# One attention-and-MLP kernel on one core: the weights are loaded and cast by GpSimd-issued DMAs instead of being staged in fp32 and cast by the engines

## The chip, the cores and the metric

The kernel runs on one core of a Trainium2 chip. The metric is the device time of one execution in microseconds (us), and less is better. A core has five engines that each run their own instruction queue in order: TensorE (PE in the profile; its weight loads are shown as PEld), VectorE (DVE), ScalarE (ACT), GpSimd (POOL) and SyncE (SP). Sixteen DMA engines move data between HBM and the on-chip memory SBUF. PSUM holds the results of matmuls.

## The reference: what is computed

Inputs are q, k, v of 8 batches x 8 heads x 576 tokens x 64 dimensions, and two weights, w_in (512 x 2048) and w_out (2048 x 512), all fp32. The output is 4608 x 512 fp32.

```python
# attention, per batch and head: two parts that are added
q_d, k_d, v_d = means over groups of 4 tokens          # 144 pooled tokens
out_up    = repeat(softmax(q_d @ k_d.T / 8) @ v_d, 4)  # every group's result for its 4 tokens
mask      = abs(i - j) < 4
out_local = softmax(where(mask, q @ k.T / 8, -1e9)) @ v
x = (out_up + out_local) as (4608 tokens, 512)
# dense part
h = x @ w_in
out = (h - tanh(h)) @ w_out
```

## The kernel before, in words

**Attention** works on pairs of heads: 8 batches x 4 pairs = 32 pairs, numbered p = 0 to 31. For a pair, q and k land in `qkn` (four buffers) and v lands in `vst` (five buffers), both fp32. `prep_v` (L351) casts v into `vw`. Two casts (L416) reorder q and k into `qr`; TensorE transposes them (L441, for p below 16) and ACT copies the result into `qk` (L445). Pooling of q and k is two additions (L457 into `half`, L462 into `qkd`). The scores come in two groups of matmuls (L476 with `qk`; L492 with the pooled `qkd`), ACT takes the exponentials (L509, L519, L522), DVE applies the mask (L512, L525). `pool_v` (L389, L391, copied out at L396 into `vd`) pools the v of two pairs at once, so it needs `vw` of both. Then `outs` (L536, L543) multiplies with v, DVE normalises (L552, L554 into `ln`), TensorE transposes back (L564 to L568), ACT copies the pooled part (L595 into `od`), and DVE adds the two parts into `xT` (L597).

**The dense part** works on 9 blocks of 512 tokens. `mm1` multiplies a block of `xT` with w_in, 16 column chunks of four matmuls each (L617); ACT takes tanh (L625), DVE subtracts (L628 into `gT`). `mm2` multiplies `gT` with w_out (L644), ACT copies out (L655), SP stores. The first block needs `xT` of all four pairs of batch 0, so no matmul of the dense part can start before the attention of pairs 0 to 3 is done.

**The weights** are cut in eight pieces of 1 MiB (fp32), four of w_in and four of w_out. Piece f of w_in is 128 x 4 x 512: 512 columns of all four row blocks, which is what chunks 4f to 4f+3 of `mm1` read. `load_w` (L324 to L346) has SP load a piece into a stage, a part of the SBUF that `gT` and `xT` will use later, and then four casts (L344) bring it as bf16 to `w_in_sb` or `w_out_sb`. Two of the w_out pieces are loaded by four DMAs each. The order of the SP queue is: q, k and v of pairs 0 to 3, the four w_in pieces, then a pair and a w_out piece in turn.

**The order of the work** is made by a planner in the kernel (`Program`). Each step is entered with an engine, an estimated time, what it reads and writes, and a priority; a step may be offered to several engines (`choice`). `order` plays this through and writes out a fixed order for each engine. So a step that is taken out or given another engine can move other steps: to another place in a queue or to another engine. The offers that matter here are the casts of v (`CAST_V`) and of q and k (`REORDER`), where POOL, ACT and, for q and k, DVE can take the first four pairs. SP has at most eight loads under way, because a load waits for the one eight places before it.

Where TensorE has nothing else to do before the dense part, the planner puts in filler matmuls (L800).

Of the kernel before, what the change touches and what calls it, by code (L numbers as in the profile page):

```python
# [8 lines left out]
FP32 = mybir.dt.float32  # L9
# [6 lines left out]
class Program:  # L16
# [18 lines left out]
    def op(self, eng, ns, fn, reads=(), writes=(), pri=0):  # L35
        i = len(self.ops)
        deps = set()
        for key in reads:
            if key in self.last_write:
                deps.add(self.last_write[key])  # L40
        for key in writes:
            if key in self.last_write:
                deps.add(self.last_write[key])
            deps.update(self.readers.get(key, ()))
        for key in reads:
            self.readers.setdefault(key, set()).add(i)
        for key in writes:
            self.last_write[key] = i
            self.readers[key] = set()
        deps.discard(i)  # L50
        self.ops.append((eng, ns, fn, deps, pri))
        self.touch.append(set(reads) | set(writes))
        return i
# [97 lines left out]
def kernel(  # L151
# [9 lines left out]
    nc = tc.nc  # L161
# [3 lines left out]
    NP = H // 2  # L165
# [23 lines left out]
    NQKN, NVST, NVW = 4, 5, 3  # L189
# [4 lines left out]
    xT = [fixed(f"xT{j}", [128, NTOK], BF16) for j in range(NP)]  # L194
    w_in_sb = fixed("w_in_sb", [128, N_DC, Dff], BF16)
    w_out_sb = fixed("w_out_sb", [128, N_FF, Dm], BF16)
    qkn = fixed("qkn", [128, 2, A9 * D], FP32, NQKN)
    vst = fixed("vst", [128, 2, NT, 64], FP32, NVST)
# [16 lines left out]
    gT = fixed("gT", [128, N_FF, 512], BF16, 2)  # L215
# [18 lines left out]
    P = Program()  # L234
    op = P.op
    V, A, T, GP = nc.vector, nc.scalar, nc.tensor, nc.gpsimd
# [45 lines left out]
    def load(ns, fn, keys, cost, pri):  # L282
        op("SP", ns, fn, writes=list(keys) + ["queue", ("q", keys[0])], pri=pri)
        op("DMA", cost, None, reads=[("q", keys[0])], writes=keys, pri=pri)
# [36 lines left out]
                op("DVE", 100, clear, writes=[("vst", s, i)], pri=-99)  # L321
            load(1000, issue, [("vst", s, i)], T_V, -30)

    def load_w(src, dst, name, f, stage, keys):  # L324

        def issue():
            if src is moe_w_in:
                nc.sync.dma_start(out=stage.rearrange("p (c f) -> p c f", c=4),
                                  in_=src[:, 512 * f:512 * f + 512].rearrange(
                                      "(c p) f -> p c f", p=128))  # L330
            else:
                rows = src.rearrange("(f p) n -> p f n", p=128)
                if isinstance(stage, list):
                    for c in range(4):
                        nc.sync.dma_start(out=stage[c], in_=rows[:, 4 * f + c, :])
                else:
                    nc.sync.dma_start(
                        out=stage.rearrange("p (c f) -> p c f", c=4),
                        in_=rows[:, 4 * f:4 * f + 4, :])
        load(600, issue, keys, T_W, -30)  # L340
        for c in range(4):
            part = stage[c] if isinstance(stage, list) else stage[:, 512 * c:512 * c + 512]
            to = dst[:, c, 512 * f:512 * f + 512] if src is moe_w_in else dst[:, 4 * f + c, :]
            P.choice([(eng, ns, lambda part=part, to=to, fn=fn: fn(out=to, in_=part))  # L344
                      for eng, ns, fn in CAST], reads=keys, writes=[(name, f, c)],
                     pri=W_PRI + f)  # L346


    def prep_v(p):
# [331 lines left out]


    M2_FIRST, T_DMA, X_DMA, NEW = 16, 16, 16, 16
    ORDER = "p0p1p2p3"
    T_QK, T_V, T_W, W_PRI, NEARLY = 800, 1000, 2850, -3, NP
    CAST = [("POOL", 700, GP.tensor_copy), ("ACT", 520, A.copy)]
    CAST_V = [[("POOL", 720, GP.tensor_copy), ("ACT", 640, A.copy)],
              [("POOL", 720, GP.tensor_copy)]]
    any3 = [("DVE", 600, V.tensor_copy), ("ACT", 650, A.copy),
# [31 lines left out]
    for p in range(NP):  # L721
        if p + 1 < NP:
            load_qk(p + 1)
        load_v(p)
    stages = []
    for g in range(2):
        t = gT[g].rearrange("p f c -> p (f c)").bitcast(FP32)
        for e in range(2):
            stages.append((t[:, 2048 * e:2048 * e + 2048],
                           [("gT", g, 8 * e + c) for c in range(8)]))  # L730
    for e in range(2):
        stages.append(([xT[c][:, 2304 + 1024 * e:3328 + 1024 * e].bitcast(FP32)
                        for c in range(4)],
                       [("x", 4 + 2 * e, c) for c in range(4)]))
    for f in range(4):
        load_w(moe_w_in, w_in_sb, "w_in", f, *stages[f])
    queue = list(ORDER)
    nl = [NP]

    def load_next():  # L740

        while queue and queue[0] != "p":
            f = int(queue.pop(0))
            load_w(moe_w_out, w_out_sb, "w_out", f, *stages[(4, 5, 2, 3)[f]])
        if queue:
            queue.pop(0)
        if nl[0] < NPAIR:
            load_qk(nl[0])
            load_v(nl[0])
            nl[0] += 1  # L750
        if not queue or "p" not in queue:
            while queue:
                f = int(queue.pop(0))
                load_w(moe_w_out, w_out_sb, "w_out", f, *stages[(4, 5, 2, 3)[f]])

    for p in range(2):
        prep_v(p)
# [74 lines left out]
```

The softmax here doesn't subtract the row's maximum and nothing guards it: scores larger than these inputs give would overflow.

## Time and profile before

| What | Value |
|---|---|
| median of 6 executions | 345.8 us (344.1 to 347.13) |
| the execution that was profiled | 344.1 us |
| its span from the first to the last instruction | 342.3 us |
| busy: PE / DVE / ACT / POOL | 319.7 / 226.5 / 227.0 / 156.3 us |
| start of the first matmul of the dense part (L617) | 30.12 us |
| casts of weights (L344) | 18 on ACT, 14 on POOL, 20.1 to 56.7 us |

The profiled execution is the fastest of the six, 1.7 us below their median, and 1.8 us of it lie outside the span. The page of the profile gives the busy time of each engine, the chain of work that ended last, groups of instructions by line, and the DMA issues. "idle before" is the time an engine had nothing to do ahead of such an instruction, with what ended that time behind an arrow. The granted TensorE clock was 0.999 of full speed in this execution.

### The profile page before, as it was taken

What the parts mean: (1) busy time and instruction counts of PE and PEld (TensorE: products, weight loads), DVE (VectorE), ACT (ScalarE), POOL (GpSimd) and SP (SyncE); (2) the same over time, 40 slices, a digit from 0 to 9 for tenths busy, and PEclk for the clock granted to TensorE, in tenths of its full rate; (3) what the DMA queues carried; (4) which work ended last, traced back from release to release, by engine and by line L of the source; (5) the groups of instructions that cost most, each with busy time, mean ns of one, the idle gap of its engine ahead of it and who ended that gap; (6) DMA issues with size and microseconds to landing.
All of it is one profiled execution on the core that took longest, in us unless ns stands there. A gap on an engine that the chain in (4) does not pass through costs nothing.

```text
span 342.3 us, 6678 instructions
## 1 busy us (share of the span) xinstructions
PE 319.7 (93%) x2458; PEld 162.9 (48%) x2502; DVE 226.5 (66%) x370; ACT 227.0 (66%) x368; POOL 156.3 (46%) x200
## 2 busy tenths in 40 slices
PE   5777999989999999999899999999999999999995
PEld 2553455545565544444345444445444444444442
DVE  4887784579989887899898867877533433343300
ACT  2886996578878949888788887895344434344411
POOL 5644655646688625678886986873000000000000
PEclk9999999999999999999999999999999999999999
DMA  7999999985769894999999999733201000100021
GB/s 200 289 388 352 335 353 303 304 259 158 192 179 227 201 226 93 246 270 242 260 211 246 232 261 211 159 85 59 57 31 63 31 31 33 61 31 34 31 92 62
DMA packets 99310, 60.72 MB, mean 177 GB/s; under 512 B 77774, under 2 KB 82382, under 8 KB 99278
## 3 DMA queue, kind: packets, MB, share of 16 engines
q1 hardware_dynamic: 99278, 60.30, 68.1%
q8 instruction: 19, 0.31, 0.4%
q14 instruction: 13, 0.11, 0.1%
HBM read 42.46 MB, written 9.44 MB: 152 GB/s over the span
## 4 chain that ended last, share of the span: by engine, by line
PE 75%; DVE 12%; DMA 4%; issue 3%; ACT 3%; SPq 2%; POOL 0%; ACTq 0%; POOLq 0%; DVEq 0%
PE ps_hy L617 32%; PE ps_hy L644 31%; DVE ln L554 3%; DMA qkn<-in_k_dram 3%; PE ps_ox L536 2%; DVE E L512 2%; PE ps_ts L476 2%; PE ps_ox L543 2%; PE ps_ts L441 2%; DVE gT L628 2%; PE ps_ox L568 1%; SPq L291 1%; PE ps_ox L389 1%; DVE qr L416 1%; DMA lT<-ln 1%
## 5 line engine op out<-in xcount | busy, mean ns | idle before, releaser
L617 PE MATMUL ps_hy<-xT,w_in_sb 128*128 128x512 bf16 x554 | 141.6, 379 | 2.7 <-DVE xT L597 1.2
L644 PE MATMUL ps_hy<-w_out_sb,gT 128*128 128x512 bf16 x557 | 139.4, 379 | 1.5 <-issue 0.8
L628 DVE TENSOR_TENSOR gT<-ps_hy,u 128x512 bf16<-128x512 f32 x144 | 96.5, 686 | 65.4 <-ACT u L625 63.6
L625 ACT ACTIVATE u<-ps_hy 128x512 f32<-128x512 f32 x144 | 84.1, 602 | 66.4 <-PE ps_hy L617 66.0
L644 PEld LDWEIGHTS <-gT 128*128 128x128 bf16 x576 | 54.4, 98 | 63.3
L617 PEld LDWEIGHTS <-w_in_sb 128*128 128x128 bf16 x576 | 52.8, 98 | 59.8 <-issue 1.3
L457 POOL TENSOR_TENSOR half<-qk 128x576 f32<-128x576 bf16 x28 | 32.4, 1158 | 18.9 <-ACT qk L445 7.3
L432 ACT COPY qk<-qT 128x576 bf16<-128x576 bf16 x32 | 38.0, 1215 | 0.0
L509 ACT ACTIVATE E<-ps_ts 128x960 bf16<-128x960 f32 x32 | 30.9, 972 | 9.4 <-PE ps_ts L476 9.1
L512 DVE TENSOR_TENSOR E<-E,mask 128x960 bf16<-128x960 bf16 x32 | 31.2, 976 | 8.2 <-ACT E L509 8.1
L554 DVE TENSOR_TENSOR ln<-ps_ox,r 128x896 bf16<-128x896 f32 x32 | 34.9, 1091 | 1.0
L416 POOL CAST qr<-qkn 128x576 bf16<-128x576 f32 x31 | 23.6, 762 | 22.5 <-PE ps_ts L441 11.0
L655 ACT COPY y<-ps_hy 128x512 f32<-128x512 f32 x36 | 21.2, 589 | 17.9 <-PE ps_hy L644 17.6
L351 POOL CAST vw<-vst 128x640 bf16<-128x640 f32 x32 | 25.4, 792 | 4.8 <-DMA vst<-in_v_dram 3.6
L416 DVE CAST qr<-qkn 128x576 bf16<-128x576 f32 x32 | 23.7, 744 | 5.3 <-DMA qkn<-in_k_dram 3.9
L536 PE MATMUL ps_ox<-vw,E 128*128 128x65 bf16 x320 | 20.2, 194 | 3.3 <-DVE E L525 1.9
L462 POOL TENSOR_TENSOR qkd<-half 128x288 bf16<-128x288 f32 x30 | 21.6, 720 | 2.7 <-DVE r L552 1.6
L372 POOL TENSOR_TENSOR v<-v 72x512 f32<-72x512 f32 x16 | 21.0, 1313 | 1.2
L536 PEld LDWEIGHTS <-E 128*128 128x128 bf16 x320 | 16.3, 98 | 11.0 <-DVE E L512 2.8
L376 POOL TENSOR_TENSOR vp<-v 72x256 bf16<-72x256 f32 x16 | 12.4, 778 | 19.7 <-PE ps_ox L543 19.6
L445 ACT COPY qk<-ps_ts 128x1152 bf16<-128x1152 bf16 x16 | 18.0, 1125 | 4.1 <-PE ps_ts L441 4.1
L476 PEld LDWEIGHTS <-qk 64*128 64x128 bf16 x320 | 10.2, 95 | 16.9 <-issue 15.2
(74 smaller groups left out, 258.8 us busy)
## 6 DMA issues: line engine op xcount, KB each, us to landing
vst<-in_v_dram SPq DMA_DIRECT2D x62, 160.0 KB, 4.5
qkn<-in_q_dram SPq DMA_DIRECT2D x32, 288.0 KB, 4.0
qkn<-in_k_dram SPq DMA_DIRECT2D x32, 288.0 KB, 5.0
out_dram<-y SPq DMA_DIRECT2D x36, 256.0 KB, 3.4
v<-in_v_dram SPq DMA_DIRECT2D x16, 288.0 KB
gT<-in_moe_w_in_dram SPq DMA_DIRECT2D x4, 1024.0 KB, 6.5
xT<-in_moe_w_out_dram SPq DMA_DIRECT2D x8, 256.0 KB, 6.7
gT<-in_moe_w_out_dram SPq DMA_DIRECT2D x2, 1024.0 KB, 8.1
```

Of the source, the lines that this page charges most:

```text
L351: P.choice([(eng, ns, lambda fn=fn: fn(out=vw[w][:, 2 * jj:2 * jj + 2, :, 0:64], in_=vst[s])) for eng, ns, fn in CAST_V[p >= NEARLY]], rea ...
L416: P.choice([(eng, ns, lambda dst=dst, srt=srt, fn=fn: fn(out=dst, in_=srt)) for eng, ns, fn in REORDER[p >= NEARLY][h]], reads=[("qkn", sn ...
L432: op("ACT", 600, lambda i=i: A.copy(out=full[:, i].rearrange("p (g a) -> p g a", a=A9), in_=qT[s].rearrange("p a (g i) -> p i g a", i=2)[: ...
L457: eng.tensor_tensor(out=half, in0=four[:, :, :, 0:2], in1=four[:, :, :, 2:4], op=ALU.add)
L509: op("ACT", 870, lambda: A.activation(out=e1, in_=ps[:, :, 0:480], func=AF.Exp, scale=SCALE), reads=ts, writes=[("E", s, 0)], pri=pri)
L512: op("DVE", 700, lambda: V.tensor_tensor(out=e1, in0=e1, in1=mask[:, 0:480].unsqueeze(1).to_broadcast([128, 2, 480]), op=ALU.mult), reads= ...
L536: T.matmul(po[:, hh, 65 * t:65 * t + 65], E[s][:, c:c + 128], vw[w][:, 2 * jj + hh, t, :], start=True, stop=True)
L554: op("DVE", 1010, lambda: V.tensor_tensor(out=ln[s].rearrange("p n (h d) -> p h n d", d=D), in0=blocks[:, :, :, 0:64], in1=r[s].unsqueeze( ...
L617: T.matmul(ps_hy[slot], w_in_sb[:, dc, fc * 128:(fc + 1) * 128], xT[dc][:, kb * 512:kb * 512 + 512], start=(dc == 0), stop=(dc == N_DC - 1))
L625: op("ACT", 490, lambda: A.activation(out=u[us], in_=ps_hy[slot], func=AF.Tanh), reads=[("hy", slot)], writes=[("u", us)], pri=-1)
L628: op("DVE", 620, lambda: V.tensor_tensor(out=gT[g][:, fc, :], in0=ps_hy[slot], in1=u[us], op=ALU.subtract), reads=[("hy", slot), ("u", us) ...
L644: T.matmul(ps_hy[slot], gT[g][:, fc, ts * 128:ts * 128 + 128], w_out_sb[:, fc, :], start=(fc == 0), stop=(fc == N_FF - 1))
```

## The change

A piece of weights is no longer staged. One DMA, issued from the GpSimd queue, reads the fp32 piece from HBM and writes it as bf16 to its place in `w_in_sb` or `w_out_sb`. The 32 casts and the 14 SP-issued loads are gone, and eight DMA issues stand in the GpSimd queue. The stages are gone, so a weight load waits for no buffer. In the planner, an issue costs POOL 1000 ns and follows the SP issue of a v load; this orders the plan only and leaves no semaphore between the two.

```diff
-    def load_w(src, dst, name, f, stage, keys):
+    def load_w(src, dst, name, f, after):
         def issue():
             if src is moe_w_in:
-                nc.sync.dma_start(out=stage.rearrange("p (c f) -> p c f", c=4),
-                                  in_=src[:, 512 * f:512 * f + 512].rearrange(
-                                      "(c p) f -> p c f", p=128))
+                GP.dma_start(out=dst[:, :, 512 * f:512 * f + 512],
+                             in_=src[:, 512 * f:512 * f + 512].rearrange(
+                                 "(c p) f -> p c f", p=128))
             else:
...
+                GP.dma_start(out=dst[:, 4 * f:4 * f + 4, :],
+                             in_=src.rearrange("(f p) n -> p f n", p=128)
+                             [:, 4 * f:4 * f + 4, :])
-        load(600, issue, keys, T_W, -30)
-        for c in range(4):
...
-            P.choice([(eng, ns, lambda part=part, to=to, fn=fn: fn(out=to, in_=part))
-                      for eng, ns, fn in CAST], reads=keys, writes=[(name, f, c)],
-                     pri=W_PRI + f)
+        keys = [(name, f, c) for c in range(4)]
+        op("POOL", 1000, issue, reads=[("q", after)], writes=keys + [("wq", name, f)],
+           pri=W_PRI)
+        op("DMA", T_W, None, reads=[("wq", name, f)], writes=keys, pri=-30)
...
     for f in range(4):
-        load_w(moe_w_in, w_in_sb, "w_in", f, *stages[f])
-    queue = list(ORDER)
+        load_w(moe_w_in, w_in_sb, "w_in", f, ("vst", (2 + f) % NVST if f < 2 else 3, 1))
...
     def load_next():
...
+        if 0 <= nl[0] - NP - 1 < 4:
+            load_w(moe_w_out, w_out_sb, "w_out", nl[0] - NP - 1,
+                   ("vst", (nl[0] - 1) % NVST, 1))
```

The planner's new order, which the compiled program shows, differs beyond the casts. In the GpSimd queue, five issues (four of w_in, one of w_out) stand in a row directly behind L462 of pair 1; then L462 of pair 2, L457 of pair 3, the sixth issue, the v cast of pair 3, the seventh, the q/k cast of pair 4, the eighth. None of the issues waits for a semaphore. Two v casts (pairs 1 and 2) and one q/k cast (pair 3) move from POOL to ACT. L457 of pair 3 moves from DVE to POOL; L462 of pair 2 moves from DVE to POOL, and that of pair 3 from POOL to DVE. On TensorE the transposes (L441) and first scores (L476) of pair 4 now stand ahead of the first L617; in the kernel before they stood behind 12 and 20 matmuls of it. On DVE, a q/k cast of pair 4 stands ahead of the mask of pair 3.

## The prediction

> **What bounds the kernel now.** I read the page's busy times first, then stretches of the span, then the instructions in order of time around the start of the dense part, then the DMA rows.
>
> ```profile
> PE 319.7 (93%) x2458; PEld 162.9 (48%) x2502; DVE 226.5 (66%) x370; ACT 227.0 (66%) x368; POOL 156.3 (46%) x200
> ...
> L617 PE MATMUL ps_hy<-xT,w_in_sb 128*128 128x512 bf16 x554 | 141.6, 379 | 2.7 <-DVE xT L597 1.2
> ```
>
> TensorE is busy 319.7 of 342.3 us, so the kernel can only win from the 22.6 us in which it is idle. Where these lie, by stretches (start and end, length, then busy time of PE, PEld, DVE, ACT, POOL):
>
> ```profile
> 0.00:30.12 30.12, 19.73 (x223) 12.23 (x227) 21.96 (x56) 19.20 (x32) 16.97 (x37) 1.00 0.99 298
> 30.12:36.00 5.88, 5.88 (x40) 2.89 (x40) 3.67 (x6) 4.37 (x8) 2.61 (x4) 1.00 1.11 345
> 36.00:48.00 12.00, 11.89 (x90) 6.31 (x91) 10.16 (x16) 11.77 (x23) 8.34 (x12) 1.00 1.11 345
> ...
> 60.00:75.00 15.00, 13.37 (x148) 7.86 (x149) 8.86 (x15) 9.26 (x16) 9.11 (x13) 1.00 0.99 287
> ```
>
> 10.4 us of the idle time lie before 30.12, where the first dense matmul starts, and 12.2 behind it. In 30.12 to 60, where ACT is almost full with casts, TensorE loses only 0.3 us. So the casts of w_out cost the end nothing, and what counts is when L617 starts. What starts it:
>
> ```profile
> 22.79 0.72 PE L389 MATMUL ps_ox<-vw,pick 128*128 128x256 bf16 x5 [0.31 <-DVE xT L597]
> ...
> 23.66 0.59 ACT L396 CAST vd<-ps_ox 128x512 bf16<-128x512 f32 x1 [0.27 <-PE ps_ox L391]
> ...
> 24.30 0.32 PE L536 MATMUL ps_ox<-vw,E 128*128 128x65 bf16 x5 [0.24 <-ACT vd L396]
> ...
> 29.31 0.76 DVE L597 TENSOR_TENSOR xT<-ps_ox,od 128x576 bf16<-128x576 bf16 x1 [0.49 <-ACT od L595]
> ...
> 30.12 2.75 PE L617 MATMUL ps_hy<-xT,w_in_sb 128*128 128x512 bf16 x12 [1.20 <-DVE xT L597]
> ```
>
> L617 waits for `xT` of pair 3, not for weights, and `xT` follows at a fixed distance from the pooling of v of pairs 2 and 3 (L389): 30.12 - 22.79 = 7.33 us. The changed GpSimd queue touches just this pooling:
>
> ```profile
> 12.45 0.66 POOL L462 TENSOR_TENSOR qkd<-half 128x288 bf16<-128x288 f32 x1
> 13.06 1.14 POOL L351 CAST vw<-vst 128x640 bf16<-128x640 f32 x1
> 14.15 1.09 POOL L416 CAST qr<-qkn 128x576 bf16<-128x576 f32 x1
> 15.63 0.72 POOL L351 CAST vw<-vst 128x640 bf16<-128x640 f32 x1 [0.39 <-DMA vst<-in_v_dram]
> 16.77 0.77 POOL L351 CAST vw<-vst 128x640 bf16<-128x640 f32 x1 [0.41 <-DMA vst<-in_v_dram]
> ```
>
> POOL has the v of pair 3 cast by 17.54, 5.2 us ahead of L389. That is the slack into which the new issues are put.
>
> **The change part by part.** *Casts removed:* 14 on POOL and 18 on ACT, 0.62 us each (median 0.61 to 0.63), 8.7 and 11.2 us. Eight of ACT's lie at 21.5 to 30.3, in gaps of ACT before L595, and the start does not wait for them. The rest lie beside a full TensorE. Worth nothing by themselves; if the cover went (a TensorE idle in 36 to 48), it would be up to 6 x 0.62 = 3.7 us.
>
> *SP's 14 issues removed:* 0.4 to 0.8 us each of a queue that nothing on the path waits for after 17 us. Pairs 4 and 5 load earlier; pair 4's q and k are used at 30.04 now, so no gain.
>
> *Eight issues on POOL.* An issue costs D. The first five begin at 13.1, behind L462 of pair 1; then come L462 (0.66), L457 (1.15, from its group's mean 1.158), issue six, and the v cast of pair 3 (0.72). This cast ends at 13.1 + 6D + 0.66 + 1.15 + 0.72 = 15.6 + 6D, and L617 can start 7.33 later: **23.0 + 6D**. Queued behind the issues are thus L462 of pair 2 (the second scores wait for it), L457 of pair 3 (DVE's L462 waits for it) and that cast (L389 waits for it); the seventh and eighth issue stand around a cast of pair 4, whose transposes are ahead of L564 on TensorE, but have 23.0 - 15.6 us more room.
>
> D is not in the trace. Lower end: 0.37 us, the shortest issue of a 1 MiB piece by SP (L337). Upper end: a w_in piece takes 6.5 us from issue to landing, and its data alone 1.05 MB / 397 GB/s (17 to 20 us) = 2.6, so at most 3.9. I take 2.0, from the row nearest to long work on this engine: POOL's longest instruction, L372, takes 1.31 us on average, and in this stretch its casts take 1.6 times their time (1.17, 1.14, 1.09 instead of 0.67 to 0.72), since DVE is busy 10.39 of the 10.90 us from 13.1 to 24.0. 1.31 x 1.6 = 2.1. With 2.0, L617 starts at 35.0: **+4.9 us**; with 0.37 POOL is no limit; with 3.9, 46.4: +16.3.
>
> The Trainium skill, page "SBUF — State Buffer", section "SBUF: two separate sides", speaks against the change: while DVE runs a two-port copy, GpSimd cannot write the descriptors of the DMAs it issues; the section after it gives 620 ns alone and 3100 ns beside such a copy. This trace shows only the slowed casts. By 3.1 the start would be 41.6 and the sum 355.4; by 0.62 POOL would not bind.
>
> *Steps that move.* ACT takes over two v casts (each 0.67 x 640/576 = 0.75) and one q/k cast (0.67). From the end of L522 of pair 0 at 13.67 its new queue up to L396 of pairs 2 and 3 is 0.75 + 0.35 + 0.69 + 0.67 + 0.60 + 1.12 + 0.75 + 1.12 + 1.95 + 0.28 + 1.02 + 0.28 + 1.02 = 10.6, so L396 starts at 24.3 instead of 23.66: L617 at 30.12 + 0.6 = **30.7** even with a short D. The two limits meet at D = 1.28. The transposes and first scores of pair 4 are done before L617 instead of among it: 0.67 + 0.38 = **-1.05 us** of TensorE work put in idle time.
>
> *Behind the start.* 1.6 us are idle at 60 to 75, where block 1 waits for batch 1 (L389 and L564 behind DVE). With ACT and POOL freed and pair 4 ahead I take half: **-0.8**; the ends are -1.6 and +1.6, the same amount lost by the new order, since nothing excludes it.
>
> *The transfers.* The engines move 1 MiB fp32 in 2.6 us now. With half the bytes written I take the same; the ends are 1.3 (bytes written alone) and 5.2 (read and write one after the other). The first piece is issued by 13.1 + 2.0, lands around 20, and the fourth by 28 at 2.6, or 37 at 5.2; L617 needs it after 12 chunks of 0.86 us and pair 4's and 5's work, at 47. Hidden.
>
> But they share the engines with the loads. v moves in 256-byte packets: 874 in 14 to 15 us, 16 engines 1.32 busy, 24 ns each; w in 2 KiB ones, 85 ns (589 in 3 us). Under D = 2.0 data flow from about 16.3 (15.1 and the 1.2 us that the first load of all needed after its issue began), and pair 3's v has left the engines by 15.6. No cost; the other end is in the rivals.
>
> **Sum:** 4.9 - 1.05 - 0.8 = +3.05: 344.1 becomes 347.1 for the profiled execution, and 345.8 becomes **348.9** for the median, in which my number is given.
>
> **The rivals.**
> *Short issue, faster.* If D is below 1.28, ACT's queue sets the start at 30.7: +0.6 - 1.05 - 0.8 = -1.25, 344.5; with all 1.6 us at 60 to 75 and half of the 3.6 idle at 125 to 175, 341.9. It decides below D = 1.49, where 23.0 + 6D - 30.12 = 1.85. For it: SP issues 640 v rows in 0.50 us and 128 q rows in 0.61, so rows need not cost; against: that is another engine.
>
> *Long issue.* D from 2.6 to 3.9: start 38.6 to 46.4, sum +6.6 to +14.4, 352.4 to 360. For it: DVE leaves POOL hardly any quiet time; against: no POOL instruction of the trace takes over 1.65 us (L372 at its slowest).
>
> *The loads are starved.* If data flow while the first piece is still being issued, at 14.5, and the engines serve the two queues a packet each, 70 v packets per engine are left and take 24 + 85 ns, or 24 + 170 if w goes 4 KiB at a time: pair 3's v is out at 22.1 or 28.1 instead of 15.6, and lands 1.2 later. Pair 4's q and k (16 packets, 96 + 85 or 96 + 170) land by 26.2 or 33.6. In the new order a DVE cast of pair 4 (wanted at 25 to 27) stands ahead of pair 3's mask, and L617 follows its end by some 5.5 us: 39 in the worse case, four more than mine: 353. In the milder case it is hidden.
>
> The skill's "DMA: Bandwidth & Descriptors", section "Queues, rings and completion order", has each engine go round the queues by whole packets, 9 to 17 descriptors being typical. Eight v rows would then stand against one w packet, v would keep over half of the engine, and this rival would cost nothing. The trace has one data queue and can't show it.
>
> That the change does not do what it says is excluded: no cast of weights is left in the compiled order.
>
> **How the numbers follow.** My case (D 1.6 to 2.6, 345.8 + 0.7 to + 6.7) 0.38; short issue 0.32; long issue 0.15; starved loads 0.15. 0.5% is 1.7 us, about what a measurement of this kernel can tell from no change. Short issue splits evenly into faster and same (0.16, 0.16); my case gives 0.05 same and 0.33 slower; long issue 0.15 slower; starved 0.01, 0.02 and 0.12. Together 0.17, 0.23, 0.60. The range goes from 343.0 (short issue with its larger gains, below which 0.08 is left) to 357.0 (D = 3.4). My own case alone has 346.5 to 352.5.
>
> **What would show it.** The v cast of pair 3 on POOL ends at 15.6 + 6D, and L389 starts right behind it; the gaps between the issues give D. L617 starts near 35. If L389 waits for DVE's L597 or L396 for ACT's own queue, the issue is short. If the wait ahead of the v cast, or ahead of DVE's q/k cast of pair 4, ends with a DMA, the loads are starved. If L617 waits for a weight DMA, the casting transfer is slow. What would make me wrong most: D, which enters six times.

## The result, and the profile after

The changed kernel takes 343.62 us (median of 31 executions, 342.39 to 347.24); the kernel before, run beside it, 346.22 us (68 executions). The ratio is 0.9939, 95% interval 0.9923 to 0.9956: **faster by 0.6%, about 2.1 us** (the medians alone differ by 2.6 us). The prediction was 348.9 us, and slower. The sign was wrong. The result lies inside the range that was given (343.0 to 357.0), near its lower end, and in the rival *Short issue, faster* (341.9 to 344.5).

The changed kernel was profiled twice. The first profile is of an execution of 346.72 us (span 344.8), the second of one of 342.34 us (span 340.5); the two lie on either side of the median, and both are used. The second execution is as fast as the fastest of the 31, as the profiled one of the kernel before was the fastest of its six, so these two are compared with each other. What before was called L617 is now L609 (`mm1`), L644 is L636 (`mm2`), L389 is L381 (`pool_v`), L396 is L388, L416 is L408, L462 is L454, L597 is L589, L351 is L343.

From the page of the first profile, the busy times:

```profile
PE 321.0 (93%) x2455; PEld 164.1 (48%) x2498; DVE 220.8 (64%) x365; ACT 220.0 (64%) x353; POOL 151.9 (44%) x196
```

ACT has lost 7.0 us of work and POOL 4.4, TensorE none. The GpSimd queue of the first profile in order of time (start, duration, line, then the wait ahead of it in brackets):

```profile
13.12 3.13 POOL L328 DMA_DIRECT2D w_in_sb<-in_moe_w_in_dram  x4
16.22 0.77 POOL L332 DMA_DIRECT2D w_out_sb<-in_moe_w_out_dram  x1
18.73 0.66 POOL L454 TENSOR_TENSOR qkd<-half 128x288 bf16<-128x288 f32 x1 [1.73 <-DVE r L544]
19.50 1.15 POOL L449 TENSOR_TENSOR half<-qk 128x576 f32<-128x576 bf16 x1
20.59 0.79 POOL L332 DMA_DIRECT2D w_out_sb<-in_moe_w_out_dram  x1
21.37 1.11 POOL L343 CAST vw<-vst 128x640 bf16<-128x640 f32 x1
```

Four issues take 3.13 us, so **D is 0.78 us, not 2.0**. After the fifth issue GpSimd even waits 1.73 us for VectorE. The v cast of pair 3 is done at 22.5. What then starts the dense part, on TensorE in the same profile:

```profile
23.52 1.25 PE L381 MATMUL ps_ox<-vw,pick 128*128 128x256 bf16 x5 [0.37 <-DVE xT L589]
...
31.64 1.67 PE L609 MATMUL ps_hy<-xT,w_in_sb 128*128 128x512 bf16 x7 [0.89 <-DVE xT L589]
```

L381 waits for VectorE, not for the v cast: GpSimd's issues are not the limit. The dense part starts at 31.64 (31.82 in the second profile), 1.5 to 1.7 us later than before. So the time is not won at the start but behind it. In the second profile the stretch from the first `mm1` to the end of the span is 340.5 - 31.82 = 308.7 us, in the kernel before 342.3 - 30.12 = 312.2. (In the first profile it is 313.2 us: TensorE is busy for only 9.42 of the 12 us from 36 to 48, and the granted clock is 0.90 in 48 to 60. What happened there is told below.) By stretches (start and end, length, busy time of PE, PEld, DVE, ACT, POOL, then granted clock, DMA share and GB/s), the second profile:

```profile
36.00:48.00 12.00, 11.81 (x101) 6.09 (x101) 9.85 (x16) 10.14 (x17) 3.53 (x5) 1.00 1.18 248
...
60.00:75.00 15.00, 14.63 (x153) 8.47 (x155) 9.56 (x16) 8.91 (x17) 9.67 (x13) 1.00 0.98 271
150.00:175.00 25.00, 23.36 (x198) 11.66 (x199) 21.33 (x33) 20.86 (x32) 20.33 (x23) 1.00 1.11 240
```

TensorE is idle for 0.37 us in 60 to 75, where it was idle for 1.63, and for 1.64 us in 150 to 175. There the kernel before had 2.60:

```profile
150.00:175.00 25.00, 22.40 (x193) 11.25 (x197) 22.63 (x34) 20.49 (x30) 19.73 (x22) 1.00 1.07 249
```

These stretches lie long after the last weight has landed, at 47 us. Whether the loads still reach them or the planner's order does it, the profiles alone don't tell; the experiments take these two apart.

### The profile page after: what moved, and what is told of

The parts are those of the page before. It is cut to its first block, busy times and chain, and to the rows that moved or that the text cites. A ratio compares the mean times of both kernels' runs of the same rounds, so it can differ in the third digit from the quotient of the medians.

```text
span 344.8 us, 6645 instructions
## 1 busy us (share of the span) xinstructions
PE 321.0 (93%) x2455; PEld 164.1 (48%) x2498; DVE 220.8 (64%) x365; ACT 220.0 (64%) x353; POOL 151.9 (44%) x196
## 4 chain that ended last, share of the span: by engine, by line
PE 72%; DMA 8%; DVE 5%; ACT 4%; issue 4%; SPq 3%; POOL 2%; ACTq 0%; POOLq 0%; DVEq 0%
PE ps_hy L636 30%; PE ps_hy L609 28%; DMA qkn<-in_k_dram 6%; PE ps_ts L468 3%; PE ps_ox L528 3%; PE ps_ts L433 2%; PE ps_ox L535 2%; DVE E L504 1%; SPq L316 1%; DVE gT L620 1%; PE ps_ox L560 1%; DMA vst<-in_v_dram 1%; ACT qk L424 1%; DMA qkn<-in_q_dram 1%; DVE qr L408 1%
## 5 line engine op out<-in xcount | busy, mean ns | idle before, releaser
L609 PE MATMUL ps_hy<-xT,w_in_sb 128*128 128x512 bf16 x552 | 141.4, 380 | 3.7 <-issue 1.7
L636 PE MATMUL ps_hy<-w_out_sb,gT 128*128 128x512 bf16 x560 | 140.0, 379 | 1.6 <-issue 1.1
L617 ACT ACTIVATE u<-ps_hy 128x512 f32<-128x512 f32 x144 | 83.8, 598 | 69.0 <-PE ps_hy L609 65.5
L636 PEld LDWEIGHTS <-gT 128*128 128x128 bf16 x576 | 54.6, 98 | 63.2
L609 PEld LDWEIGHTS <-w_in_sb 128*128 128x128 bf16 x576 | 52.9, 98 | 60.5 <-issue 2.7
L449 POOL TENSOR_TENSOR half<-qk 128x576 f32<-128x576 bf16 x29 | 33.3, 1149 | 39.8 <-ACT qk L437 28.4
L504 DVE TENSOR_TENSOR E<-E,mask 128x960 bf16<-128x960 bf16 x32 | 27.0, 846 | 10.1 <-ACT E L501 9.8
L408 POOL CAST qr<-qkn 128x576 bf16<-128x576 f32 x30 | 21.5, 718 | 16.4 <-DMA qkn<-in_k_dram 9.8
L408 DVE CAST qr<-qkn 128x576 bf16<-128x576 f32 x32 | 23.6, 737 | 7.5 <-DMA qkn<-in_k_dram 7.5
L343 POOL CAST vw<-vst 128x640 bf16<-128x640 f32 x30 | 25.5, 851 | 2.6 <-DMA vst<-in_v_dram 2.6
L528 PE MATMUL ps_ox<-vw,E 128*128 128x65 bf16 x320 | 21.0, 197 | 3.1 <-DVE E L517 1.5
L454 POOL TENSOR_TENSOR qkd<-half 128x288 bf16<-128x288 f32 x30 | 20.6, 688 | 3.0 <-DVE r L544 1.7
L528 PEld LDWEIGHTS <-E 128*128 128x128 bf16 x320 | 17.0, 100 | 10.3 <-DVE E L504 2.2
L368 POOL TENSOR_TENSOR vp<-v 72x256 bf16<-72x256 f32 x16 | 11.6, 726 | 14.9 <-PE ps_ox L535 13.8
```

The source lines that it names most:

```text
L343: P.choice([(eng, ns, lambda fn=fn: fn(out=vw[w][:, 2 * jj:2 * jj + 2, :, 0:64], in_=vst[s])) for eng, ns, fn in CAST_V[p >= NEARLY]], rea ...
L408: P.choice([(eng, ns, lambda dst=dst, srt=srt, fn=fn: fn(out=dst, in_=srt)) for eng, ns, fn in REORDER[p >= NEARLY][h]], reads=[("qkn", sn ...
L449: eng.tensor_tensor(out=half, in0=four[:, :, :, 0:2], in1=four[:, :, :, 2:4], op=ALU.add)
L504: op("DVE", 700, lambda: V.tensor_tensor(out=e1, in0=e1, in1=mask[:, 0:480].unsqueeze(1).to_broadcast([128, 2, 480]), op=ALU.mult), reads= ...
L528: T.matmul(po[:, hh, 65 * t:65 * t + 65], E[s][:, c:c + 128], vw[w][:, 2 * jj + hh, t, :], start=True, stop=True)
L609: T.matmul(ps_hy[slot], w_in_sb[:, dc, fc * 128:(fc + 1) * 128], xT[dc][:, kb * 512:kb * 512 + 512], start=(dc == 0), stop=(dc == N_DC - 1))
```

## The experiments

All ratios are to the kernel before, run beside each kernel, with 95% intervals.

### A second look at the changed kernel

No edit.

> The changed kernel once more, for a second profile of it. The first profiled execution took 346.7 us, against a median of 343.6, with a granted clock of 0.90 to 0.96 in three stretches before 60 us. Theory A, the low clock is particular to that execution: an execution near 343.5 us has a clock of 1.00 throughout, its L609 of block 0 starts by 31.0, and the idle time of TensorE at 36 to 48 stays (about 2.5 us), since it comes from loads. Theory B, the clock is low in every execution of this kernel: the clock column again shows 0.90 to 0.96 before 60 us.

Measured: 342.34 us. TensorE was busy for 11.81 of the 12 us from 36 to 48, where it had only 9.42 in the first profile. What it missed there in the first profile was a load, on DVE and TensorE in order of time:

```profile
46.80 0.75 DVE L408 CAST qr<-qkn 128x576 bf16<-128x576 f32 x1 [3.24 <-DMA qkn<-in_k_dram]
...
47.70 1.12 PE L433 MATMUL ps_ts<-ident,qr 128*128 128x128 bf16 x9 [1.98 <-DVE qr L408]
```

So starved loads do cost the changed kernel time, but not in each execution. Neither theory holds as a whole: the fast execution has a low clock too, its L609 starts at 31.82 and not by 31.0, and the idle time at 36 to 48 is nearly gone (0.19 us), while the clock from 36 to 60 is at 1.00. What both profiles share is a fall of the granted clock, here the first one by stretches of 2 us (the clock is the third number from the end):

```profile
22.00:24.00 2.00, 0.82 (x9) 0.47 (x8) 2.00 (x4) 1.02 (x4) 1.50 (x3) 0.80 1.20 199
24.00:26.00 2.00, 1.75 (x13) 1.15 (x13) 1.69 (x4) 0.65 (x2) 1.01 (x2) 0.50 1.22 196
```

L381 falls into it: its five matmuls span 1.25 us for the 0.72 of before, and from L381 to L609 it takes 8.12 us for the 7.33.

### The price of an issue by itself: D set to 2.0

Two copies that nobody needs stand behind each issue; the order of all else is that of the changed kernel.

```diff
+        def padded():
+            issue()
+            for c in range(2):
+                GP.tensor_copy(out=junk[c], in_=mask[:, 0:512])
-        op("POOL", 1000, issue, reads=[("q", after)], ...
+        op("POOL", 1000, padded, reads=[("q", after)], ...
```

> after with two 128x512 copies on GpSimd behind each of the eight issues, into a scratch tile that nobody reads (0.656 us each in old_copies): an issue with its copies then costs 0.78 + 1.31 = 2.09 us, close to the 2.0 that the prediction took. By the prediction's working (v cast of pair 3 ends at 15.6 + 6D, first mm1 at 23.0 + 6D) the cast ends at 28.1 and the first mm1 starts at 35.5, 3.9 us behind after's 31.6, and the time is 346 to 348.5 us, ratio 1.001 to 1.008. If D was the only step that failed, that is what comes. If GpSimd isn't on this path at all, the start stays at 31.6 to 32.5 and the time at after's 343.6.

Measured: 346.52 us, ratio 0.9994 (0.9962 to 1.0026). The GpSimd queue and then TensorE, in order of time:

```profile
12.87 0.90 POOL L329 DMA_DIRECT2D w_in_sb<-in_moe_w_in_dram  x1
13.78 1.70 POOL L339 COPY junk<-mask 128x512 bf16<-128x512 bf16 x2
...
24.65 0.78 POOL L333 DMA_DIRECT2D w_out_sb<-in_moe_w_out_dram  x1
25.43 1.25 POOL L339 COPY junk<-mask 128x512 bf16<-128x512 bf16 x2
26.64 0.71 POOL L348 CAST vw<-vst 128x640 bf16<-128x640 f32 x1
...
27.40 1.23 PE L386 MATMUL ps_ox<-vw,pick 128*128 128x256 bf16 x5 [1.26 <-POOL vw L348]
...
35.56 1.67 PE L614 MATMUL ps_hy<-xT,w_in_sb 128*128 128x512 bf16 x7 [0.89 <-DVE xT L594]
```

The five issues ahead of L459 take 9.95 us with their copies (12.87 to 22.82), the sixth 2.03: D is 2.00 on average. The working of the prediction then gives 15.6 + 12.0 = 27.6 for the end of the v cast and 35.0 for the first `mm1`; the trace has 27.35 and 35.56. **The formula 23.0 + 6D holds within 0.6 us, and in it D was the wrong term.** (The 0.6 us are two differences: the cast ends 0.25 us earlier, and from L386 to L614 it takes 8.16 us for 7.33, with the granted clock at 0.50 from 22 to 30.) The run also shows the second thing that was wrong, what happens behind the start. With the start at 35.56, which is 5.4 us later than before, the kernel is no slower than before. From its start to its end it takes 308.1 us, again 4.0 less than before, where the prediction allowed 1.85.

### Is it the work that is gone, or the order? Before's order with the new loads

The planner of before is left as it is, with its weight loads and casts in the plan. But what is emitted is the DMA on GpSimd, and no casts. TensorE, DVE and ACT (but for the casts) have exactly the order of before.

```diff
-        load(600, issue, keys, T_W, -30)
+        load(600, None, keys, T_W, -30)
+        op("POOL", 0, issue, reads=[("q", keys[0])], pri=W_PRI)
         for c in range(4):
-            P.choice([(eng, ns, lambda ...: fn(out=to, in_=part)) ...
+            P.choice([(eng, ns, None) for eng, ns in CAST], reads=keys,
+                     writes=[(name, f, c)], pri=W_PRI + f)
```

> Before's own order of the instructions on TensorE, VectorE and ScalarE, with the weights loaded as in after: eight GpSimd-issued casting DMAs in place of before's staged loads, no casts emitted, the loads of SP without the weights among them. What it leaves of the change out is the new order that the planner makes of the freed time. Two theories of the 3.8 us that after gains behind the dense start (block 0's first tanh to the last y took 307.3 us in before and 303.5 in after's second profile). Relief: the time comes from the work that is gone (casts from ACT and GpSimd, weights from SP's queue and from the staging buffers) in whatever order: then ratio 0.990 to 0.995, first tanh to last y 303 to 305 us. Order: the time comes from the planner's new order, which puts pair 4's transposes and scores ahead of the dense start and shifts the pairs behind it: then first tanh to last y 306 to 308 us, ratio 0.997 to 1.003.

Measured: 349.04 us, ratio **1.0079** (1.0048 to 1.0111). Without the new order the change makes the kernel slower by 2.7 us. First `mm1` at 31.52, and from there to the end 347.7 - 31.52 = 316.2 us. The two stretches from above:

```profile
60.00:75.00 15.00, 13.69 (x142) 7.75 (x140) 9.01 (x15) 9.47 (x15) 8.23 (x11) 1.00 0.98 283
150.00:175.00 25.00, 22.33 (x189) 10.68 (x184) 21.80 (x31) 20.34 (x32) 19.68 (x23) 1.00 1.08 246
```

TensorE is idle for 1.31 and 2.67 us, much as before (1.63 and 2.60). Relief by the work that is gone has fallen.

### The casts alone

As the kernel just above, with 32 copies of 128 x 512 in the places of before's casts, from a tile that is ready from the start into one that nobody reads (0.62 us on ACT, 0.66 on POOL).

```diff
-            P.choice([(eng, ns, None) for eng, ns in CAST], reads=keys, ...
+            P.choice([("POOL", 700, lambda: GP.tensor_copy(out=junk[0], in_=mask[:, 0:512])),
+                      ("ACT", 520, lambda: A.copy(out=junk[1], in_=mask[:, 0:512]))],
+                     reads=keys, ...
```

> As old_order, with 32 copies of 128x512 put where before had its casts (same place in the order, same engines), from a tile that has been ready since the start into a scratch tile that nobody reads: the engines' work of the casts is back, without any wait for a weight. It answers what the casts alone cost. Relief by the engines: slower than old_order by 0.3 to 0.8% (1 to 3 us), near before. Casts worth nothing by themselves (the prediction's step): within 0.2% of old_order.

Measured: 348.99 us, ratio 1.0085 (1.0053 to 1.0116), against 1.0079 without them. **The engine time of the casts costs nothing that these intervals (0.3% to either side) can show**, as the prediction said. These copies wait for nothing, where before's casts wait for landings.

### The other corner: the new order with the old loads

The plan of the changed kernel is kept to the last instruction on TensorE and DVE. Beside it, the weights are loaded by SP into the stages of before, and 32 casts (16 on ACT, 16 on POOL) are put behind the landings; both are emitted by their planned time, outside the plan.

```diff
-        op("POOL", 1000, issue, reads=[("q", after)], ...
-        op("DMA", T_W, None, reads=[("wq", name, f)], writes=keys, pri=-30)
+        i = op("POOL", 1000, None, reads=[("q", after)], ...
+        d = op("DMA", T_W, None, reads=[("wq", name, f)], writes=keys, pri=-30)
+        P.aside.append((i, d, T_W, issue, cast))
...
```

> after's own order of all instructions on TensorE and VectorE (and of all but the casts on ScalarE and GpSimd), with the weights loaded as before loads them: staged fp32 loads in SP's queue and 32 casts (16 on ScalarE, 16 on GpSimd), put behind the landings and ahead of the first use. It is the other corner beside old_order, which took 1.0079 of before with after's loads and before's order. Order theory (the gain comes from the planner's new order, the new transfers themselves cost some): faster than before, ratio 0.985 to 0.995. Pairing theory (each order fits only the loads that it was planned for): as slow as old_order or slower, ratio 1.003 to 1.015. Relief theory (the gain comes from work that is gone): 1.000 or above, but old_order speaks against it already.

Measured: 342.78 us, ratio **0.9914** (0.9879 to 0.9950). This kernel, which has SP's loads, the stages and all 32 casts, is faster than before by as much as the changed kernel or more. Its stretches:

```profile
60.00:75.00 15.00, 14.73 (x167) 8.91 (x169) 9.87 (x16) 10.16 (x18) 9.45 (x13) 1.00 1.06 296
150.00:175.00 25.00, 23.21 (x195) 11.54 (x198) 20.13 (x30) 20.24 (x30) 20.50 (x24) 1.00 1.11 244
```

0.27 and 1.79 us idle, as in the changed kernel. The four corners:

| | loads of before | GpSimd's casting loads |
|---|---|---|
| order of before | 1.0000 | 1.0079 (1.0048 to 1.0111) |
| order of after | 0.9914 (0.9879 to 0.9950) | 0.9939 (0.9923 to 0.9956) |

The order is worth -0.9% with the old loads and -1.4% with the new ones. The new loads are worth +0.8% in the old order and +0.25% in the new one, the latter within the intervals. In neither order do they gain anything. The two kernels of the lower row were not run beside each other, and their intervals overlap, so it stays open which of them is the faster.

### Is the new order better for a reason, or a draw?

One number in the planner of the changed kernel is made truer: an issue costs 780 ns.

```diff
-        op("POOL", 1000, issue, reads=[("q", after)], ...
+        op("POOL", 780, issue, reads=[("q", after)], ...
```

> after with one number changed: the planner is told 780 ns for an issue on GpSimd, as measured, for 1000. Nothing else is edited, but the planner makes another order of it. If an order made with the truer price is the better one, 341 to 343.5 us (ratio 0.985 to 0.992). If the order that a small change brings is no more than another draw, anywhere from 342 to 349 us.

Measured: 348.68 us, ratio 1.0058 (1.0024 to 1.0091). The truer price makes an order that is 1.2% slower. Its stretches:

```profile
60.00:75.00 15.00, 12.99 (x140) 7.83 (x139) 9.25 (x15) 9.46 (x15) 8.24 (x12) 1.00 1.05 296
150.00:175.00 25.00, 22.16 (x181) 10.70 (x182) 22.57 (x32) 20.46 (x32) 19.65 (x23) 1.00 1.06 246
```

2.01 and 2.84 us idle. It starts `mm1` at 32.26, close to the changed kernel, and has the transposes and first scores of pair 4 ahead of it too. So it loses behind the start.

The planned time of the q and k loads of pairs 4 to 6 is raised, since they land late beside the weights:

```diff
-            load(500, issue, [("qkn", s, i)], T_QK, -30)
+            load(500, issue, [("qkn", s, i)], T_QK + 1200 * (NP <= p < 7), -30)
```

> after with the planned cost of the q and k loads of pairs 4 to 6 raised by 1200 ns each (they land later than planned, beside the weights). The planner then puts TensorE's and VectorE's work on them further back. If the waits for starved loads cost after its time (3.24 us of VectorE's for pair 6's k in its profile at 46.8, 0.37 to 1.3 us of TensorE's between 36 and 48), 341 to 343 us, ratio 0.984 to 0.991. If the order is again only another draw, 342 to 349 us; it tells the same from cost780.

Measured: 351.54 us, ratio 1.0131 (1.0088 to 1.0174), with 2.13 and 3.49 us idle in the two stretches. First `mm1` at 31.75. Again an order made with truer times, and again slower. Two further orders with the new loads, below, with other issue times, gave 1.0108 and 1.0039. **Of six orders that were run with the new loads and no added work, five are slower than before, and the one that came with the change is the one that is faster.** It looks like a draw: prices made truer did not lead the planner to a faster order. Filling the two stretches is not enough by itself, either. The two spread kernels below are idle there for 0.16 and 2.99 us and for 0.40 and 1.34 us, and are slower than before all the same: the first starts `mm1` late, at 34.47; the second is idle for 2.61 us from 36 to 60, where the kernel before is for 0.32, with the clock at 0.86 in 48 to 60. So the stretches tell where the order that came with the change gains. Why it gains there is not shown.

### Spreading the issues

The issues are released at set times of the plan instead of following v loads.

```diff
-        op("POOL", 1000, issue, reads=[("q", after)], ...
+        op(("W", name, f), W_AT[name][f], None, writes=[("w_go", name, f)])
+        op("POOL", 800, issue, reads=[("w_go", name, f)], ...
...
+    W_AT = {"w_in": [11000, 11000, 16000, 20000], "w_out": [26000, 30000, 34000, 38000]}
```

> The changed kernel with the eight issues spread over the GpSimd queue: two w_in pieces at 13 us, the third and fourth behind v casts, the w_out pieces one behind the other between the steps of pairs 4 and 5, so that at most two or three pieces are under way. Theory S (one packet of weights for one packet of q, k or v starves the loads of pairs 5 and 6 until 47 us): with fewer pieces under way TensorE's idle time at 36 to 48 falls from 2.6 to under 1 us and the ratio to the kernel before goes to 0.980 to 0.989. Rival, the engines are simply full up to 60 us whatever the order: the idle time moves but stays, ratio 0.991 to 0.998.

Measured: 351.4 us, ratio 1.0108 (1.0069 to 1.0146). The execution that was profiled is the fastest of its seven, 348.39 us. In it TensorE's idle time at 36 to 48 is 0.11 us, as theory S asked, but the time is not what S asked. The clock stayed at 1.00 from 12 to 32, but `mm1` started at 34.47, behind `xT` of pair 3, and VectorE shows why:

```profile
32.90 0.75 DVE L409 CAST qr<-qkn 128x576 bf16<-128x576 f32 x1 [3.43 <-DMA qkn<-in_k_dram]
33.57 0.75 DVE L590 TENSOR_TENSOR xT<-ps_ox,od 128x576 bf16<-128x576 bf16 x1
```

In this order the cast of pair 5's q and k stands ahead of the addition that `mm1` waits for, and its load was late. This is the prediction's rival *The loads are starved*, one pair later. The next kernel moves that cast behind the addition, with the same edit of `load_qk` as in the kernel above.

> spread_a with the planned cost of the q and k loads of pairs 4 to 6 raised by 1200 ns each, which moves VectorE's cast of pair 5's q and k behind the last addition into xT of pair 3 (in spread_a it stood ahead of it and waited 3.43 us for its load). If that one wait made spread_a slower, the first mm1 starts at 30.2 to 31.5 us in place of 34.5, first tanh at 31.5 to 33, and the time falls from spread_a's 348.4 profiled to 343 to 346 (ratio 0.990 to 0.999). If the loads that the weights starve hold up something else in its place, the first tanh stays at 34 or later and the ratio above 1.003.

Measured: 348.05 us, ratio 1.0039 (1.0011 to 1.0068). The first `mm1` starts at 32.42, two us earlier than in the kernel it was made from. So taking that wait away brought two us of the three to four that were expected, and another starved load had taken its place, the v of pair 3 on GpSimd:

```profile
22.95 0.72 POOL L344 CAST vw<-vst 128x640 bf16<-128x640 f32 x1 [3.26 <-DMA vst<-in_v_dram]
```

### Casts back, and the old loads in GpSimd's queue

Two earlier kernels answer less: the first has yet another order, and in the second GpSimd waits for landings. In the first, the changed kernel has 32 unneeded copies, from the weights that have landed:

```diff
+        for c in range(4):
+            P.choice([("POOL", 700, lambda part=part: GP.tensor_copy(out=junk[0], in_=part)),
+                      ("ACT", 520, lambda part=part: A.copy(out=junk[1], in_=part))],
+                     reads=[(name, f, c)], pri=W_PRI + f)
```

> The changed kernel with 32 copies put back: each piece of weights, once landed, is copied in four parts (128x512) on POOL or ACT as the planner chooses, into a scratch tile that nobody reads. So the load of the engines is that of the kernel before, while the loads stay as changed. Theory C, the gain comes from the casts taken off ACT and POOL: the ratio to the kernel before goes back to 0.998 to 1.010, as 20 us of work return to stretches where pairs 4 to 7 are prepared. Theory L, the gain comes from the loads (weights out of SP's queue and out of the stages): the ratio stays at 0.992 to 0.997.

Measured: ratio 1.0048 (1.0012 to 1.0085). Beside the changed kernel's 0.9939 this looked as if the casts cost 1.1%, but the copies also made the planner choose another order. The dense part starts at 35.82. One copy stands ahead of the v cast of pair 3, but what L387 (`pool_v`) waits for at 26.00 is VectorE's `xT`, for 1.40 us. The copies that wait for nothing (above) cost nothing that could be seen, so this loss is hardly that of the casts' engine time; it was not taken apart further.

In the second, before's staged fp32 loads are issued by GpSimd, casts kept:

```diff
-                nc.sync.dma_start(out=stage.rearrange(...), in_=...)
+                GP.dma_start(out=stage.rearrange(...), in_=...)
-        load(600, issue, keys, T_W, -30)
+        op("POOL", 1000, issue, reads=[("q", after)], writes=list(keys) + [("wq", name, f)], ...
```

> The kernel before with one thing changed: the staged fp32 loads are issued by GpSimd instead of SP, at the places that the change gives them; stages and casts stay. Theory C: no gain from that alone, ratio 1.000 to 1.015, since POOL now waits for landings ahead of the v cast of pair 3. Theory L: part of the gain appears, ratio 0.993 to 0.998.

Measured: 359.98 us, ratio 1.0384 (1.0337 to 1.0430), first `mm1` at 42.44. GpSimd's queue in order of time:

```profile
25.06 0.54 POOL L335 DMA_DIRECT2D xT<-in_moe_w_out_dram  x1 [3.79 <-DMA gT<-in_moe_w_in_dram]
...
31.12 0.54 POOL L335 DMA_DIRECT2D xT<-in_moe_w_out_dram  x1 [2.49 <-DMA gT<-in_moe_w_in_dram]
31.65 0.62 POOL L346 CAST w_in_sb<-gT 128x512 bf16<-128x512 f32 x1
32.21 0.73 POOL L353 CAST vw<-vst 128x640 bf16<-128x640 f32 x1
```

Here issues wait for earlier weights to land, and behind them a cast and then the v cast of pair 3. The issues of the changed kernel wait for nothing, which is why they could be put into a queue that the start depends on.

### Fillers against the fall of the clock

Four filler matmuls at each gap that the planner finds on TensorE between 12 and 28 us of its plan.

```diff
-            if self.start[i] - last > 350:
+            if self.start[i] - last > (100 if 12000 < self.start[i] < 28000 else 350):
...
+                n = 4 if 12000 < self.start[i] < 28000 else 0
-                fill[i] = (name, int(0.75 * room / slow))
+                fill[i] = (name, max(n, int(0.75 * room / slow)))
```

> after with four filler matmuls in place of one or two at each gap that the planner finds on TensorE between 12 and 28 us of its plan (12 more in all). After's two profiles show the granted clock at 0.50 in 24 to 26 us, behind stretches of 2 us in which TensorE was busy for 0.82 to 0.85 us, and pair 3's transposes there took 1.67 us for 0.99. If the idle time brings the clock down and the fillers hold it up, PEclk stays at 0.9 or more in 22 to 28, the first mm1 starts about 0.7 us earlier (31.0 for 31.7), ratio to before 0.990 to 0.994, about 0.002 below after's. If the gaps that bring it down are others (18 to 20, where no PSUM bank is free for a filler), the clock falls as before and the time is after's or up to 1 us longer.

Measured: 344.32 us, ratio 0.9945 (0.9915 to 0.9975), the changed kernel's within the interval. The clock fell nevertheless, and earlier:

```profile
22.00:24.00 2.00, 1.77 (x8) 0.72 (x9) 2.00 (x5) 0.87 (x2) 1.31 (x3) 0.50 1.22 199
24.00:26.00 2.00, 2.00 (x11) 1.14 (x9) 1.06 (x3) 0.41 (x1) 0.58 (x1) 0.70 1.22 195
```

Behind four fillers at 15.06 the next begin at 22.58, when the clock is already down. Whether the idle time of 18 to 22 brings it down, where the plan has no PSUM bank free for a filler, or something else, stays open.

## Why the prediction was wrong

**D, the failed step.** "I take 2.0": measured 0.78 on average (0.74 to 0.91). The rows that it was worked out from were computing instructions of GpSimd, slowed beside a busy VectorE; an issue is not one. At D = 0.78 the formula gives 27.7 for the first `mm1`, so GpSimd's issues don't bind. (The v cast itself ended at 22.5 and not at 15.6 + 6 x 0.78 = 20.3, mainly because L454 waited 1.73 us for VectorE, a wait that the formula lacks; L381 came 1 us after the cast all the same.) With D = 2.00 put in, the start came at 35.56 for the 35.0 of the working, and the time rose by 346.52 - 343.62 = 2.9 us, or 1.9 us by the ratios (0.9994 and 0.9939). This is a third to a half of the miss: the prediction had +3.1 us, measured was -2.6 by the medians and -2.1 by the ratio.

**The other limit** was 1 us short, and it did not lie where the rival had it. The short-issue rival put the start at 30.7, by ACT's longer queue up to L396; it was 31.64 and 31.82. L381 waited for DVE's `xT`, one of the signs named for a short issue. But L388 (L396 of before) waited for TensorE, not for ACT's own queue:

```profile
25.02 0.59 ACT L388 CAST vd<-ps_ox 128x512 bf16<-128x512 f32 x1 [0.95 <-PE ps_ox L383]
```

In the second profile the chain that leads to `mm1` does pass through a v cast that ACT had taken over (14.23 to 14.97); what it costs was not measured. L381 itself starts 0.7 us later than L389 did before (23.52 for 22.79). From L381 to L609 it takes 8.12 us for 7.33, and 0.6 of these 0.8 us lie between L381 and L388, where the clock is down; the prediction had it at full speed, as in the profile before.

**Behind the start**, the prediction had -1.05 and -0.8. The -1.05 came: 17 matmuls of pair 4 are ahead of `mm1`. But they don't decide the sign, since the two slower orders made with truer times have them too. From the first `mm1` to the end of the span the changed kernel's second profile is 3.5 us shorter than that of before, and the kernel with D at 2.0 4.0 us, where the two terms together made 1.85. The -0.8 was a term of the right kind and too small: 1.26 us less idle in 60 to 75, and 0.96 less in 150 to 175, for which I allowed nothing in the sum and half of it only in the larger gain of the rival. By "with ACT and POOL freed" I gave the wrong reason: the same gaps close with all casts in place (0.27 and 1.79 us idle) and stay open without them (1.31 and 2.67). What in the new order closes them stays open.

**Casts removed worth nothing:** right, 1.0085 with copies and 1.0079 without.

**The transfers are hidden:** right for the start of `mm1`, which no weight held up. But the price was wrong. From the page of the first profile, the issues with their medians from issue to landing:

```profile
w_in_sb<-in_moe_w_in_dram POOLq DMA_DIRECT2D x4, 512.0 KB, 12.3
w_out_sb<-in_moe_w_out_dram POOLq DMA_DIRECT2D x4, 512.0 KB, 20.7
```

A piece lands 12 to 21 us after its issue, where it took 6.5 to 8.1, and the last weight data flow until 47.5 us (46.7 in the second profile). The first `mm2` starts at 53.97 (50.25), so 6.5 and 3.5 us are left; in neither profile does TensorE wait for a weight.

**Starved loads**, the rival with 0.15, is right in its mechanism: the two queues move as many packets each. It did not hold up the first `mm1` of the changed kernel. The DMA rows of 26 to 28 us (packets, MB, share of 16 engines):

```profile
q0 software_dynamic: 320, 0.31, 91.9%
q1 hardware_dynamic: 321, 0.08, 30.1%
```

320 packets against 321. A weight packet takes 0.919 x 2 us x 16 / 320 = 92 ns, a load's packet 30 ns; so of the time that the packets take, three quarters are those of the weights. The Trainium skill's page "DMA: Bandwidth & Descriptors", section "Queues, rings and completion order", has an engine go round the queues by packets of typically 9 to 17 descriptors; read as I read it, several v rows would have stood against one weight packet. Counted in the rows that the trace shows, it is one against one on average; the counts don't tell whether the queues take turns row by row or by groups of as many rows. I gave the rival the right mechanism and the wrong place: VectorE's cast of pair 4 ahead of pair 3's mask (at 24.22) waited for no load. The waits came at pair 6 in the first profile, at pair 5 and at pair 3 in the spread kernels.

The Trainium skill's page "SBUF — State Buffer", section "SBUF: two separate sides", was weighed against the change. The section behind it, "A bandwidth-pool intuition that's wrong (but worth ruling out)", has about 620 ns for a GpSimd-issued DMA alone and 3100 ns beside a VectorE copy; these are times of a DMA, and the prediction tried them as times of an issue in the queue. The eight issues took 0.74 to 0.91 us, with VectorE busy for 2.00 us of 12 to 14. The last one (24.27 to 25.01) stood beside a cast of VectorE (24.22 to 24.96) and took 0.74. No run here shows the slow case.

**The sign.** Short issue had 0.32, and half of it was booked as no change, since the gain behind the start was priced at 1.85. For the second profile the sum is +1.7 at the start and -3.5 behind it. Of the 3.5, 1.5 are less idle time of TensorE (2.2 less in the two stretches, 0.7 more elsewhere) and 2.0 less busy time; pair 4's work is 1.05 of the latter, the rest is not resolved. That 343.62 lies between the 341.9 and 344.5 of the short-issue rival is in part luck: its start was 1 us too early, and its gain behind the start too small. Nothing in the profile before could show which order the planner would draw; the order itself could be read, but no rule that tells a faster order from a slower one was found here.

What stays open: why the new loads cost 0.8% in the old order. Its profile starts `mm1` 1.4 us later than that of before and loses 4.0 us more behind the start. There the clock is at 0.65 in 32 to 36, and the first twelve matmuls take 4.35 us for 2.75, which makes 1.6 of the 4.0; what the clock does differs between the profiles. Another 1.1 lie at 195 to 200, long after the weights: TensorE is idle there for 1.19 us, waiting for VectorE's `ln`, where the kernel before is for 0.06; the kernel with the copies has the same 1.19. VectorE is late because one of its additions into `xT` (L579, at 192.91) takes 2.42 us, where the same one took 0.78 in the kernel before (L586, at 188.72). GpSimd runs L365 and L450 beside it, from 192.56 to 195.22; in the kernel before the addition was all but over when L365 (there L372) began. Whether the two engines hold each other up there was not tested. The remaining 1.3 us were not found. Over the 12 executions the clock of the kernel with before's order averages 0.986, that of the kernel before beside it 0.993. A part of the 0.8% may be the clock, though among the 12 the time does not follow it (348.35 us at 0.979, 349.2 at 0.995).

## What to carry to other kernels

Where a planner makes the order, each edit is two changes: what it says, and another order. Run the four corners (old and new order, old and new work) before one of them gets the credit; here the work lost up to 0.8%, and the order won 0.9 to 1.4%, a draw that two truer planning prices lost again. A DMA issue that waits for nothing is cheap to have in the queue of a computing engine (0.78 us here), one that waits for a landing is not (359.98 us). And large packets in a second queue take the DMA engines' time packet by packet from small ones: look at who loads small rows at that time, and which engine has a step that waits for them ahead of the critical one.

## What the runs showed of the hardware that was not expected

- The software and the hardware DMA queue moved packet for packet (320 and 321 in 2 us), though a packet of the one takes 92 ns and of the other 30.
- A casting packet (2 KiB of fp32 read, 1 KiB of bf16 written) of a weight takes 92 ns beside the other queue; a 2 KiB packet of the staged fp32 load took 85 ns in one queue, and a 4 KiB packet of it in GpSimd's queue, beside SP's, 167 ns (0.932 x 6 us x 16 / 537, from 22 to 28 us). Halving the bytes written gained nothing.
- In most profiles here the granted clock falls to 0.50 for some us within the first 40 us, at different places; in the profile of the kernel before it did not (0.999), but 35 other executions of that kernel average 0.993. A group of five matmuls went from 0.72 to 1.25 us in it.
- Issuing a 1 MiB piece by GpSimd took 0.90 to 0.91 us for the first piece of a kernel, where it is shown by itself, and 0.74 to 0.79 for the others, a quarter of a piece 0.54 to 0.56; a busy VectorE made no difference that shows.
